# Long-run loads for x and w_out, weights of the first matmul read with a stride of four, and a reordered start

## The chip, the cores and the metric

The kernel runs on one core of a Trainium2 chip. The metric is the device time of one execution in microseconds, and the median of several executions is compared. A profile comes from one such execution.

The core has a matrix engine (TensorE, PE in the profile, with its weight loads apart as PEld), a vector engine (VectorE, DVE), a scalar engine (ScalarE, ACT), GpSimd (POOL) and a queue engine (SyncE, SP). SP and POOL issue DMAs here, and only those of POOL change the type on the way ("casting DMAs").

## The reference, cut to what matters

```python
# x: 8 x 4096 x 192, weight: 8 heads x 7 taps, w_in: 192 x 2048, w_out: 2048 x 192, all float32
w = softmax(weight)                               # over the 7 taps (with 1e-9 in the divisor)
conv[b, s, d] = sum_k w[head(d), k] * x_padded[b, s + k, d]     # 6 zero rows before each sequence
h = conv.reshape(32768, 192) @ w_in
out = maximum(0.01 * h, h) @ w_out                # 32768 x 192, float32
```

A short causal convolution with one set of taps for each of 8 heads is followed by a two-layer network with a leaky rectifier.

## The kernel before, in words

**Layout.** Two batch rows are worked on at once: they are r = 2p + e, with e = 0 on partitions 0 to 63 and e = 1 on 64 to 127. The 192 channels are three chunks of 64. So `xt` holds x with channels on partitions, three chunks and a halo of 16 columns, in bf16. A block is 512 positions of such a pair of rows, and there are 32 blocks (`NBLK`). The first five blocks are worked in two halves of 256 positions each (`HT`), the other 27 whole; `groups` is the list of these pieces. "Half 0" to "half 3" below are the first four groups; halves 0 and 1 are block 0, halves 2 and 3 are block 1.

**Getting x.** For most blocks, `load_x` brings x as bf16 into `x_bf` by six casting DMAs of POOL, one for each chunk and row, and `transpose_x` turns it by DMA transposes on SP into `xt`. The first four halves go another way, since the start cannot wait for that. `load_first` (L108) brings float32 rows by SP into `x_nat`, with one DMA for each of the two rows, 128 rows to a slab and one row of 768 bytes to a partition and slab. `cast_first` (L126) makes bf16 of it on DVE or ACT, `transpose_first` (L141) turns it on TensorE in twelve pieces into PSUM (`ptr`), and `evac_first` (L155) copies it to `xt`.

**The convolution.** `conv_jobs` makes the taps on DVE: for each chunk one multiply (L174) and six multiply-adds (L180), into `yt`. For half 0, chunks 0 and 1, and half 1, chunk 0, `pe_conv_jobs` does it on TensorE instead: 28 matmuls with diagonal weights (L199), two of them for each of 7 taps and two parts of the taps' precision. A scaling takes them out of PSUM, on ACT (`act_scale`, L328) for half 0 and on DVE (L205) for half 1.

**The two matmuls.** `mm1` makes one "unit" u: 12 matmuls of 256 columns (two feature groups of 128) in a half, or 6 of 512 in a whole block. Each pair runs on the two halves of the array's rows. ACT applies the rectifier and writes `g` (L372). The tile `ph` has two buffers, so TensorE can be two units ahead of ACT. `mm2_slot` makes two matmuls of the second product from `g` and `w_out` (L391); a fixed quota of slots follows each pair of units ("step" j), for groups that are already done. Outputs are taken from PSUM by `evac_o` (L438) and stored by SP. Two outputs are built together in two rounds with a change of array halves between them; the copy of the previous pair's second output stands as a seal between the rounds (`seal_round`). PSUM tiles for `ptr`, the convolution's `acc` and the outputs `po` share four buffers.

**Order.** The order of each engine's instructions is the order of the program text (`tc.manual_schedule()`). In half 0 (i = 0) there is no second product yet; there the taps of half 1 run, and the loads of halves 2 and 3 are let go behind the activations of units 0 and 6, by a dependence that is put in by hand. In half 1 (i = 1) half 3 is cast on ACT behind units 2 and 3 and turned after step 1. POOL's later loads wait behind a small copy (`pjunk`, L494) that reads the last `g` of half 0:

```python
if i == 1 and j == 1:
    nc.gpsimd.tensor_copy(out=pjunk, in_=g[0][0:1, NFC - 1, 1, HT - 1 : HT])
    load_x(2)
```

At the start SP issues the taps and the four loads of halves 0 and 1. POOL builds the selection matrix, then issues w_in in four casting DMAs (L236) and w_out in one (L241). TensorE is kept busy with matmuls of zeros (`warm`, L248) while it waits.

Of the kernel before, what the change touches and what calls it, by code (L numbers as in the profile page):

```python
# [9 lines left out]
FP32 = mybir.dt.float32  # L10
BF16 = mybir.dt.bfloat16
# [3 lines left out]
def kernel(  # L15
# [8 lines left out]
    nc = tc.nc  # L24

    B, S, D = x.shape
# [8 lines left out]
    CH = 64  # L35
    NCH = D // CH
    ST = 512
    SUB = ST // 128
    HT = ST // 2
    HS = SUB // 2  # L40
    NFC = F // 128
    NB = S // ST
    NBLK = (B // 2) * NB
    NHALF = 5
    NPEC = 2

# [15 lines left out]
    groups = [(b, h * HT, HT) for b in range(NHALF) for h in range(2)]  # L62
# [39 lines left out]

    def load_first(q, after=None):
        t = stage_pool.tile([128, 2, HS, D], FP32, name="x_nat")
        for e in range(2):
            ins = nc.sync.dma_start(  # L108
                out=t[:, e, :, :],
                in_=x[e, q * HT : (q + 1) * HT, :].rearrange("(c p) d -> p c d", p=128),  # L110
            )
            if after is not None and e == 0:
                tc.add_manual_dep(
                    ins.ins, after.ins.name,
                    mybir.DependencyInfo(
                        mybir.DependencyClass.Sync, mybir.DependencyReason.DATA
                    ),
                    reason="leave the DMA engines to the weights",
                )
        x_nat[q] = t  # L120

    def cast_first(q, e, copy):
        if q % 2 == 0 and e == 0:
            x_bf[q // 2] = xb_pool.tile([128, NCH, SUB, 2, CH], BF16, name="x_bf")
        h = q % 2
        copy(  # L126
            out=x_bf[q // 2][:, :, h * HS : (h + 1) * HS, e, :],
            in_=x_nat[q][:, e, :, :].rearrange("p s (c k) -> p c s k", c=NCH),
        )

# [2 lines left out]
    def transpose_first(q):  # L133
        ts = [
            psum_o.tile([128, HS, NCH, CH], BF16, name=f"ptr{i}", tag="po") for i in range(2)
        ]
        for s in range(HS):
            for c in range(NCH):
                for i in range(2):
                    ps = slice(i * CH, (i + 1) * CH)  # L140
                    nc.tensor.transpose(  # L141
                        out=ts[i][:, s, c, :],
                        in_=x_bf[q // 2][ps, c, (q % 2) * HS + s, :, :].rearrange(
                            "p e k -> p (e k)"
                        ),
                        identity=ident[ps, ps],
                    )
        ptr[q] = ts

    def evac_first(q, *copies):  # L150
        dst = xt[0][:, :, HALO + q * HT : HALO + (q + 1) * HT].rearrange(
            "p c (s i k) -> p i s c k", s=HS, i=2
        )
        for i, t in enumerate(ptr.pop(q)):
            copies[i](out=dst[:, i], in_=t)  # L155
# [78 lines left out]
    for fs in (slice(0, F // 2), slice(F // 2, F)):  # L234
        for e in range(2):
            nc.gpsimd.dma_start(  # L236
                out=w_in[e * CH : (e + 1) * CH, :, fs],
                in_=moe_w_in[:, fs].rearrange("(c p) f -> p c f", p=CH),
            )
    w_out = const_pool.tile([128, NFC, D], BF16)  # L240
    nc.gpsimd.dma_start(out=w_out, in_=moe_w_out.rearrange("(c p) d -> p c d", p=128))  # L241


    wa = psum_h.tile([128, 2, ST], FP32, name="warm", tag="ph")

    def warm(n):
        for _ in range(n):
            nc.tensor.matmul(  # L248
                out=wa[:, 0, 0:HT], lhsT=zero[:, 0:128], rhs=zero, start=True, stop=True
            )  # L250


# [102 lines left out]
    def mm1(grp, u):  # L355
        blk, t0, T = grp
        y = yt[blk]
        nf = ST // T
        ph = psum_h.tile([128, 2, ST], FP32, name="ph", tag="ph")
        for i in range(nf):  # L360
            f = nf * u + i
            for c in range(NCH):
                for e in range(2):
                    ps = slice(e * CH, (e + 1) * CH)
                    nc.tensor.matmul(  # L365
                        out=ph[:, e, i * T : (i + 1) * T],
                        lhsT=w_in[ps, c, f * 128 : (f + 1) * 128],
                        rhs=y[ps, c, t0 : t0 + T],
                        start=(c == 0),
                        stop=(c == NCH - 1),  # L370
                    )
        act = nc.scalar.activation(  # L372
            out=g[blk][:, nf * u : nf * (u + 1), :, t0 : t0 + T],
            in_=ph.rearrange("p e (i t) -> p i e t", i=nf),
            func=mybir.ActivationFunctionType.Prelu, alpha=0.01,
        )
        return act
# [66 lines left out]
            )  # L444
        return ins

    pjunk = const_pool.tile([1, 1], BF16)
    slot, avail = 0, 0
    for i, grp in enumerate(groups):
        blk, t0, T = grp  # L450
        steps = T // 64
        if t0 == 0:
            g[blk] = g_pool.tile([128, NFC, 2, ST], BF16, name="g", tag="g")
        quota = (avail - slot) // steps

        if i == 0:
            ahead = []
        else:
            ahead = conv_jobs(groups[i + 1]) if i + 1 < len(groups) else []
        per = -(-len(ahead) // steps)  # L460
        for j in range(steps):
            for u in range(2 * j, 2 * j + 2):
                act = mm1(grp, u)
                if i == 0 and u == 0:
                    pe_ahead, evac_y = pe_conv_jobs(groups[1], 0)
                    ahead = conv_jobs(groups[1], range(1, NCH))
                    per = len(ahead)
                if i == 0 and u == 3:
                    for job in pe_ahead:
                        job()  # L470
                if i == 0 and u in (0, 6):
# [24 lines left out]
            if i == 2 and j == 1:  # L496
                transpose_x(2)
            for job in jobs:
                job()
            if i == 1 and j == 1:  # L500
                transpose_first(3)
                evac_first(3, nc.vector.tensor_copy, nc.vector.tensor_copy)

            last_half = t0 + T == ST
            if j == steps // 4 and last_half:
                load_x(blk + 3)
            if j == steps // 2 and last_half and blk > 0:
                transpose_x(blk + 2)
        avail += 2 * T // 128 * NFC
# [36 lines left out]
```

## Time and profile before

| what | value |
|---|---|
| time, median of 3 runs | 695.6 us (695.6 to 696.04) |
| the profiled execution, time | 695.24 us |
| the profiled execution, span from first to last instruction | 693.5 us |
| granted TensorE clock | 1.000 |
| TensorE busy | 683.7 us, 99% of the span |
| VectorE, ScalarE, GpSimd busy | 543.9, 516.4, 139.7 us |
| DMA | 54.39 MB in 184015 packets |

The span is shorter than the execution's time by what lies before the first and after the last instruction. Busy shares are means over stages with different limits, so a stage must be read by itself: which wait ends last there. A row of a view names the line, the engine, the operation, the tiles written and read, and how often (x); in brackets stands how long the engine sat idle before it and what ended that. DMA-issuing instructions are not counted as busy.

### The profile page before, as it was taken

What the parts mean: (1) busy time and instruction counts of PE and PEld (TensorE: products, weight loads), DVE (VectorE), ACT (ScalarE), POOL (GpSimd) and SP (SyncE); (2) the same over time, 40 slices, a digit from 0 to 9 for tenths busy, and PEclk for the clock granted to TensorE, in tenths of its full rate; (3) what the DMA queues carried; (4) which work ended last, traced back from release to release, by engine and by line L of the source; (5) the groups of instructions that cost most, each with busy time, mean ns of one, the idle gap of its engine ahead of it and who ended that gap; (6) DMA issues with size and microseconds to landing.
All of it is one profiled execution on the core that took longest, in us unless ns stands there. A gap on an engine that the chain in (4) does not pass through costs nothing.

```text
span 693.5 us, 26049 instructions
## 1 busy us (share of the span) xinstructions
PE 683.7 (99%) x11778; PEld 539.4 (78%) x11778; DVE 543.9 (78%) x1005; ACT 516.4 (74%) x577; POOL 139.7 (20%) x195
## 2 busy tenths in 40 slices
PE   7999999999999999999999999999999999999997
PEld 5899998677777777777777777777777777777777
DVE  7899998977878787878787878877878878777812
ACT  6788888977777777777777777777777777777771
POOL 3632201502222202222112222102222022000000
PEclk9999999999999999999999999999999999999999
DMA  9995535935566345565355564545655365222112
GB/s 169 122 103 81 88 66 79 92 75 74 67 93 81 68 82 69 73 87 82 68 80 77 75 82 82 77 67 80 80 82 81 70 82 68 62 60 62 45 36 70
DMA packets 184015, 54.39 MB, mean 78 GB/s; under 512 B 148320, under 2 KB 183136, under 8 KB 183904
## 3 DMA queue, kind: packets, MB, share of 16 engines
q0 software_dynamic: 97936, 14.17, 30.3%
q1 hardware_dynamic: 85968, 38.56, 22.4%
q8 instruction: 92, 1.51, 1.0%
q14 instruction: 19, 0.16, 0.1%
HBM read 29.88 MB, written 25.17 MB: 79 GB/s over the span
## 4 chain that ended last, share of the span: by engine, by line
PE 93%; DMA 3%; DVE 2%; ACT 1%; POOL 0%; issue 0%; SPq 0%; POOLq 0%; DVEq 0%
PE po L391 48%; PE ph L365 45%; DVE yt L180 2%; DMA w_in<-in_moe_w_in_dram 1%; DMA x_nat<-in_x_dram 1%; DMA xt<-x_bf 1%; ACT g L372 0%; POOL sel L226 0%; DVE yt L174 0%; ACT x_bf L126 0%; POOL w_in L236 0%; PE ptr L141 0%; DVE x_bf L126 0%; SPq L441 0%; POOL sel L224 0%
## 5 line engine op out<-in xcount | busy, mean ns | idle before, releaser
L372 ACT ACTIVATE g<-ph 128x1024 bf16<-128x1024 f32 x512 | 496.2, 1021 | 156.2 <-PE ph L365 155.8
L180 DVE SCALAR_TENSOR_TENSOR yt<-xt,wk,yt 128x512 bf16<-128x512 bf16 (+1 forms) x648 | 442.3, 683 | 17.6
L391 PEld LDWEIGHTS <-g 64*128 64x128 bf16 (+1 forms) x8064 | 352.2, 94 | 45.3 <-issue 0.2
L391 PE MATMUL po<-w_out,g 64*128 64x192 bf16 (+1 forms) x8064 | 382.7, 243 | 0.0
L365 PE MATMUL ph<-yt,w_in 64*128 64x512 bf16 (+1 forms) x3552 | 379.3, 347 | 2.7 <-DMA w_in<-in_moe_w_in_dram 1.1
L365 PEld LDWEIGHTS <-w_in 64*128 64x128 bf16 x3552 | 186.5, 94 | 98.1 <-issue 4.6
L77 POOL DMA_DIRECT2D x_bf<-in_x_dram x180 | 133.7, 774 | 422.1 <-DMA xt<-x_bf 419.7
L438 DVE COPY o_sb<-po 128x192 f32<-128x192 f32 x216 | 77.1, 357 | 121.5 <-PE po L391 115.5
L174 DVE TENSOR_SCALAR yt<-xt,wk 128x512 bf16<-128x512 bf16 (+1 forms) x108 | 37.5, 347 | 2.0 <-DMA xt<-x_bf 1.9
L438 ACT COPY o_sb<-po 128x192 f32<-128x192 f32 x40 | 12.8, 320 | 1.9
L248 PE MATMUL warm<-zero 128*128 128x256 bf16 x24 | 4.8, 348 | 1.1 <-DVE junk L216 1.1
L199 PE MATMUL acc<-xt,diag 64*64 64x256 bf16 x84 | 5.2, 270 | 0.5 <-DVE xt L155 0.5
L199 PEld LDWEIGHTS <-diag 64*64 64x64 bf16 x84 | 4.3, 106 | 1.2 <-DVE xt L155 0.8
L303 ACT ACTIVATE diag<-ident,whm 128x64 bf16<-128x64 bf16 x14 | 3.5, 335 | 1.9 <-DVE whm L289 1.9
L248 PEld LDWEIGHTS <-zero 128*128 128x128 bf16 x24 | 2.4, 118 | 2.1 <-DVE junk L216 1.1
L494 POOL COPY pjunk<-g 1x1 bf16<-1x1 bf16 x1 | 0.2, 176 | 16.0 <-ACT g L372 16.0
L126 DVE CAST x_bf<-x_nat 128x384 bf16<-128x384 f32 x5 | 2.3, 454 | 1.4 <-DMA x_nat<-in_x_dram 1.4
L141 PE MATMUL ptr<-ident,x_bf 64*128 64x64 bf16 x48 | 1.4, 191 | 1.8 <-ACT x_bf L126 0.9
L141 PEld LDWEIGHTS <-x_bf 64*128 64x128 bf16 x48 | 1.0, 95 | 2.8 <-ACT x_bf L126 2.2
L236 POOL DMA_DIRECT2D w_in<-in_moe_w_in_dram x4 | 2.6, 660 | 0.0
L155 DVE COPY xt<-ptr 128x384 bf16<-128x384 bf16 x7 | 2.2, 351 | 0.5 <-PE ptr L141 0.4
L253 ACT ACT_TABLE_LOAD x1 | 1.3, 1283 | 0.8 <-PEq L530 0.8
(35 smaller groups left out, 12.9 us busy)
## 6 DMA issues: line engine op xcount, KB each, us to landing
out_dram<-o_sb SPq DMA_DIRECT2D x128, 192.0 KB, 2.1
x_bf<-in_x_dram POOLq DMA_DIRECT2D x180, 64.0 KB, 3.4
x_nat<-in_x_dram SPq DMA_DIRECT2D x8, 192.0 KB, 4.0
w_in<-in_moe_w_in_dram POOLq DMA_DIRECT2D x4, 384.0 KB, 9.7
xt<-x_bf SPq DMA_TRANSPOSE x90, 2.6
w_out<-in_moe_w_out_dram POOLq DMA_DIRECT2D x1, 768.0 KB, 16.3
w<-in_weight_dram SPq DMA_DIRECT2D x1, 0.2 KB
```

What stands on the lines that cost most here:

```text
L77: nc.gpsimd.dma_start(out=t[:, c, :, e, :], in_=src[2 * rp + e, :, :, c * CH : (c + 1) * CH],)
L141: nc.tensor.transpose(out=ts[i][:, s, c, :], in_=x_bf[q // 2][ps, c, (q % 2) * HS + s, :, :].rearrange("p e k -> p (e k)"), identity=ident ...
L174: lambda s=src, d=dst, c=c: nc.vector.tensor_scalar_mul(d, s, wk[:, c, 0:1])
L180: lambda s=src, d=dst, c=c, k=k: nc.vector.scalar_tensor_tensor(out=d, in0=s, scalar=wk[:, c, k : k + 1], in1=d, op0=mybir.AluOpType.mult, ...
L199: lambda k=k, p=p, a=a, e=e, ps=ps: nc.tensor.matmul(out=acc[ps, :T], lhsT=diag[c][ps, p, k, :], rhs=xt[0][ps, c, a : a + T], start=(k == ...
L236: nc.gpsimd.dma_start(out=w_in[e * CH : (e + 1) * CH, :, fs], in_=moe_w_in[:, fs].rearrange("(c p) f -> p c f", p=CH),)
L248: nc.tensor.matmul(out=wa[:, 0, 0:HT], lhsT=zero[:, 0:128], rhs=zero, start=True, stop=True)
L303: nc.scalar.activation(out=diag[c][:, 1, k, :], in_=ident2, func=mybir.ActivationFunctionType.Copy, scale=whm[:, c, 1, k : k + 1],)
L365: nc.tensor.matmul(out=ph[:, e, i * T : (i + 1) * T], lhsT=w_in[ps, c, f * 128 : (f + 1) * 128], rhs=y[ps, c, t0 : t0 + T], start=(c == 0) ...
L372: act = nc.scalar.activation(out=g[blk][:, nf * u : nf * (u + 1), :, t0 : t0 + T], in_=ph.rearrange("p e (i t) -> p i e t", i=nf), func=my ...
L391: return nc.tensor.matmul(out=po[m], lhsT=g[b][ps, fc, e, s * 128 : (s + 1) * 128], rhs=w_out[ps, fc, :], start=start, stop=stop,)
L438: ins = copy(out=o_sb[:, n % 2, :], in_=po.pop(n))
```

## The change

The rows of x for halves 0 to 3 are dealt to partitions two at a time: partition p takes positions 2p and 2p + 1, which lie side by side in memory (1536 bytes), and one DMA brings both batch rows. Evacuation to `xt` then writes every second column. Halves 0 and 1 still come by SP as float32 and are cast. Half 2 comes by one casting DMA of POOL into `x_rows` and is turned in 24 smaller pieces. Half 3 comes by six casting DMAs into `x_half3` in the layout that the transposes read. POOL's queue now holds, in order, w_in, half 2, w_out, half 3 and block 2, with no wait between them.

w_out is dealt four rows at a time (`RUN = 4`): partition p takes the features 512 c + 4 p + i, which lie side by side in memory (3072 bytes). To match, `mm1` picks the columns of w_in with a stride of four.

Half 1's casts move from DVE to ACT, behind the two scalings of half 0. Its transposes move from before the first unit to behind it, its 28 taps on TensorE are spread over units 2 to 5, and its scaling moves to ACT. Half 2 is turned behind unit 6. Half 3 is turned after step 2 of half 1, not after step 1. A few warm matmuls are added. The helper's argument `after`, the copy to `pjunk` and the casts of halves 2 and 3 go.

```diff
+    RUN = 4
...
-    def load_first(q, after=None):
-        t = stage_pool.tile([128, 2, HS, D], FP32, name="x_nat")
-        for e in range(2):
-            ins = nc.sync.dma_start(
-                out=t[:, e, :, :],
-                in_=x[e, q * HT : (q + 1) * HT, :].rearrange("(c p) d -> p c d", p=128),
-            )
-            if after is not None and e == 0:
-                tc.add_manual_dep(
...
-        x_nat[q] = t
+    x_half = {
+        q: const_pool.tile([128, NCH, HS, 2, CH], BF16, name=f"x_half{q}") for q in (0, 1, 3)
+    }
+    x_rows = const_pool.tile([128, 2, HS, D], BF16, name="x_rows")
+
+    def load_first(q):
+
+        rows = x[0:2, q * HT : (q + 1) * HT, :].rearrange("e (p s) d -> p e (s d)", s=HS)
+        if q < 2:
+            x_nat[q] = stage_pool.tile([128, 2, HS, D], FP32, name="x_nat")
+            nc.sync.dma_start(out=x_nat[q].rearrange("p e s d -> p e (s d)"), in_=rows)
+        elif q == 2:
+            nc.gpsimd.dma_start(out=x_rows.rearrange("p e s d -> p e (s d)"), in_=rows)
+        else:
+            for c in range(NCH):
+                for e in range(2):
+                    nc.gpsimd.dma_start(
+                        out=x_half[q][:, c, :, e, :],
+                        in_=rows[:, e].rearrange("p (s d) -> p s d", s=HS)[
+                            :, :, c * CH : (c + 1) * CH
+                        ],
+                    )
...
-                    nc.tensor.transpose(
-                        out=ts[i][:, s, c, :],
-                        in_=x_bf[q // 2][ps, c, (q % 2) * HS + s, :, :].rearrange(
-                            "p e k -> p (e k)"
-                        ),
-                        identity=ident[ps, ps],
-                    )
+                    if q != 2:
+                        nc.tensor.transpose(
+                            out=ts[i][:, s, c, :],
+                            in_=x_half[q][ps, c, s, :, :].rearrange("p e k -> p (e k)"),
+                            identity=ident[ps, ps],
+                        )
+                        continue
+                    for e in range(2):
+                        nc.tensor.transpose(
+                            out=ts[i][e * CH : (e + 1) * CH, s, c, :],
+                            in_=x_rows[ps, e, s, c * CH : (c + 1) * CH],
+                            identity=ident[ps, ps],
+                        )
...
-            "p c (s i k) -> p i s c k", s=HS, i=2
+            "p c (i k s) -> p i s c k", s=HS, i=2
...
+    load_first(2)
+
+
     w_out = const_pool.tile([128, NFC, D], BF16)
-    nc.gpsimd.dma_start(out=w_out, in_=moe_w_out.rearrange("(c p) d -> p c d", p=128))
+    nc.gpsimd.dma_start(
+        out=w_out.rearrange("p (c i) d -> p c i d", i=RUN),
+        in_=moe_w_out.rearrange("(c p i) d -> p c i d", p=128, i=RUN),
+    )
+    load_first(3)
+    load_x(2)
...
-    warm(5)
+    warm(7)
+    warm(1, 128)
...
-    for n, job in enumerate(conv_jobs(groups[0], range(NPEC, NCH))):
-        if n in (4, 5):
-            cast_first(1, n - 4, nc.vector.tensor_copy)
+    for job in conv_jobs(groups[0], range(NPEC, NCH)):
         job()
     for c in range(NPEC):
         pe_jobs, evac_y = pe_conv_jobs(groups[0], c)
         for job in pe_jobs:
             job()
         evac_y(act_scale)
+        cast_first(1, c, nc.scalar.copy)
         if c == 0:
             warm(2)
-    transpose_first(1)
-    evac_first(1, nc.vector.tensor_copy, nc.vector.tensor_copy)
...
-                        lhsT=w_in[ps, c, f * 128 : (f + 1) * 128],
+                        lhsT=w_in[
+                            ps, c, bass.DynSlice(f // RUN * RUN * 128 + f % RUN, 128, RUN)
+                        ],
...
-                act = mm1(grp, u)
+                mm1(grp, u)
                 if i == 0 and u == 0:
+                    transpose_first(1)
+                    evac_first(1, nc.vector.tensor_copy, nc.vector.tensor_copy)
                     pe_ahead, evac_y = pe_conv_jobs(groups[1], 0)
                     ahead = conv_jobs(groups[1], range(1, NCH))
                     per = len(ahead)
-                if i == 0 and u == 3:
-                    for job in pe_ahead:
+                if i == 0 and 2 <= u <= 5:
+
+                    n = len(pe_ahead) // 4
+                    for job in pe_ahead[(u - 2) * n : (u - 1) * n]:
                         job()
-                if i == 0 and u in (0, 6):
-                    load_first(2 + u // 6, act)
-                if i == 1 and u in (2, 3):
-                    cast_first(3, u - 2, nc.scalar.copy)
+                if i == 0 and u == 5:
+                    evac_y(act_scale)
+                if i == 0 and u == 6:
+                    transpose_first(2)
...
             if i == 0 and j == 3:
-                evac_y(nc.vector.tensor_scalar_mul)
-                for e in range(2):
-                    cast_first(2, e, nc.vector.tensor_copy)
-                transpose_first(2)
                 evac_first(2, nc.vector.tensor_copy, nc.vector.tensor_copy)
-            if i == 1 and j == 1:
-
-                nc.gpsimd.tensor_copy(out=pjunk, in_=g[0][0:1, NFC - 1, 1, HT - 1 : HT])
-                load_x(2)
...
-            if i == 1 and j == 1:
+            if i == 1 and j == 2:
                 transpose_first(3)
                 evac_first(3, nc.vector.tensor_copy, nc.vector.tensor_copy)
```

More of the change, by code (lines that the diff above doesn't have):

```diff
@@ L101, in new_xt @@
         nc.vector.memset(xt[rp][:, :, 0:HALO], 0.0)
-    def load_first(q, after=None):
-        t = stage_pool.tile([128, 2, HS, D], FP32, name="x_nat")
-        for e in range(2):
-            ins = nc.sync.dma_start(
-                out=t[:, e, :, :],
-                in_=x[e, q * HT : (q + 1) * HT, :].rearrange("(c p) d -> p c d", p=128),
-            )
-            if after is not None and e == 0:
-                tc.add_manual_dep(
-                    ins.ins, after.ins.name,
-                    mybir.DependencyInfo(
-                        mybir.DependencyClass.Sync, mybir.DependencyReason.DATA
-                    ),
-                    reason="leave the DMA engines to the weights",
-                )
-        x_nat[q] = t
+    x_half = {
[18 more added lines that the diff above has]
+                    )
     def cast_first(q, e, copy):
-        if q % 2 == 0 and e == 0:
-            x_bf[q // 2] = xb_pool.tile([128, NCH, SUB, 2, CH], BF16, name="x_bf")
-        h = q % 2
         copy(
-            out=x_bf[q // 2][:, :, h * HS : (h + 1) * HS, e, :],
+            out=x_half[q][:, :, :, e, :],
             in_=x_nat[q][:, e, :, :].rearrange("p s (c k) -> p c s k", c=NCH),
@@ L140, in transpose_first @@
                     ps = slice(i * CH, (i + 1) * CH)
-                    nc.tensor.transpose(
-                        out=ts[i][:, s, c, :],
-                        in_=x_bf[q // 2][ps, c, (q % 2) * HS + s, :, :].rearrange(
-                            "p e k -> p (e k)"
-                        ),
-                        identity=ident[ps, ps],
-                    )
+                    if q != 2:
[11 more added lines that the diff above has]
+                        )
         ptr[q] = ts
@@ L239, with warm @@
             )
+    load_first(2)
     w_out = const_pool.tile([128, NFC, D], BF16)
-    nc.gpsimd.dma_start(out=w_out, in_=moe_w_out.rearrange("(c p) d -> p c d", p=128))
+    nc.gpsimd.dma_start(
[4 more added lines that the diff above has]
+    load_x(2)
     wa = psum_h.tile([128, 2, ST], FP32, name="warm", tag="ph")
-    def warm(n):
+    def warm(n, cols=HT):
         for _ in range(n):
             nc.tensor.matmul(
-                out=wa[:, 0, 0:HT], lhsT=zero[:, 0:128], rhs=zero, start=True, stop=True
+                out=wa[:, 0, 0:cols], lhsT=zero[:, 0:128], rhs=zero[:, 0:cols],
+                start=True, stop=True,
             )
@@ L285 @@
     select(wps_l, 2)
-    warm(5)
+    warm(7)
+    warm(1, 128)
     new_xt(0)
@@ L445, in evac_o @@
         return ins
-    pjunk = const_pool.tile([1, 1], BF16)
     slot, avail = 0, 0
```

## The prediction

> **What bounds the kernel now.** I read the page's first part, then busy time by stretch, then the chain that ended last and the timeline of the first 35 us, which give the place and size of every wait.
>
> ```profile
> PE 683.7 (99%) x11778; PEld 539.4 (78%) x11778; DVE 543.9 (78%) x1005; ACT 516.4 (74%) x577; POOL 139.7 (20%) x195
> ```
> ```profile
> 33.80:118.00 84.20, 84.20 (x1800) 79.66 (x1796) 79.06 (x168) 72.23 (x97) 20.20 (x28) 1.00 0.61 84
> 136.00:677.00 541.00, 541.00 (x9108) 413.97 (x9106) 418.76 (x733) 401.48 (x415) 95.59 (x129) 1.00 0.49 73
> ```
> In the stretches the columns are length, then busy us of PE, PEld, DVE, ACT, POOL, clock and DMA. TensorE has no hole at all from 33.8 to 118 and from 136 to 677; between them it lacks 0.5 us (17.51 of 18), and the tail after 677 is the last output. So the time moves in two ways only: the dense stream starts earlier or later, or its own pace changes.
>
> ```profile
> 3.65 8.95 DMA w_in<-in_moe_w_in_dram
> 12.64 0.84 PE ph L365 x11
> 13.51 1.03 ACT g L372
> 14.97 6.26 DMA x_nat<-in_x_dram
> 21.25 0.44 DVE x_bf L126
> 26.58 0.40 ACT x_bf L126
> 27.91 0.41 ACT x_bf L126
> 28.36 0.35 PE ptr L141 x12
> ```
> This is the chain (start, length, what). The first matmul waits until w_in lands at 12.6; half 2's x is let go only behind the first g (13.5) and lands at 21.2; half 3's cast stands in ACT's line between two g's.
>
> ```profile
> 14.58 1.75 PE L365 MATMUL ph<-yt,w_in 64*128 64x256 bf16 x24 [0.46 <-ACT g L372]
> 16.26 1.72 PE L199 MATMUL acc<-xt,diag 64*64 64x256 bf16 x28
> 19.86 1.75 PE L365 MATMUL ph<-yt,w_in 64*128 64x256 bf16 x24 [0.46 <-ACT g L372]
> 21.91 1.63 PE L365 MATMUL ph<-yt,w_in 64*128 64x256 bf16 x24
> 28.36 0.35 PE L141 MATMUL ptr<-ident,x_bf 64*128 64x64 bf16 x12 [0.86 <-ACT x_bf L126]
> 33.81 0.93 PE L365 MATMUL ph<-yt,w_in 64*128 64x256 bf16 x14
> 6.09 0.60 DVE L318 TENSOR_SCALAR rsum<-wraw 128x3 f32<-128x3 f32 x1
> 33.52 0.49 DVE L174 TENSOR_SCALAR yt<-xt,wk 128x256 bf16<-128x256 bf16 x1
> ```
> Half 1's matmuls start at 21.91, half 2's at 33.81. DVE finishes half 2's y at 33.52, so there DVE is only 0.3 us ahead. That moment, 33.81, is my yardstick: everything after it is dense and follows it one for one.
>
> [...] No strided weight is in the trace before; it shows 94 ns per load, and that loads keep up with the second matmul's pace of 1.32 us for 16 pairs, 82 ns. [...] the 128x3 multiply at 6.09 took 0.60 us and ended as POOL's w_out issue did (5.51 + 1.20), while the two-input taps took the same 3.09 us for six with POOL issuing and without. [...] from 5 to 6 us x's packets take 38.0% of the engines and w_in's 59.5%.
>
> **The change, part by part.**
> *Loads of halves 0, 1* (SP): four issues become two, runs 768 to 1536 bytes. x still occupied 0.38 us of all engines after 5.0 us, when w_in's packets begin. I expect x to be through by then: w_in lands 0.45 earlier, 12.15 (bounds 0 and 0.9: nothing, or all of x's remaining share plus fewer stragglers). POOL issues w_in as before.
> *Casts of half 1* leave DVE (0.42 + 0.43, so chunk 2 of y is ready at 10.9, not 11.72) for ACT (2 x 0.5, one after each scaling). ACT's last scaling ends at 11.18 + 0.47 = 11.65, its second cast at 12.17. All are before 12.15 or level with it: hidden by w_in's landing. Three more warm matmuls and two small ones are covered by waits (TensorE idles from 5.1 to 5.9); the small one ahead of the first selection may cost 0.05.
> *Half 1's transposes* move behind the first unit of matmuls. Before, DVE could begin half 1's taps at 12.29. Now: 12.15 + 12 matmuls at 54.5 ns (24 took 1.31) = 12.80, transposes 0.35 = 13.15, two evacuations 0.62 = 13.80. Behind DVE's wait stand half 1's taps, half 2's evacuation and half 2's taps.
> *Half 1's taps on TensorE*: one block of 28 (1.72 us) held ACT from 17.39 to 18.78. Four parts of 0.43 alternate with units of 0.65. Two units ahead of ACT is the limit (two ph buffers), so ACT runs nearly through: 12.85 + 8 x 0.97 + 0.45 for the scaling it takes from DVE = 21.1, perhaps 21.2 with half 2's 24 transposes (12 cost 0.35; I take 0.5, bounds 0.3 and 1.2).
> *Half 1's matmuls*: y's chunk 2 comes from DVE at 13.80 + 6.72 (12.29 to 19.01) = 20.55; the second unit needs ACT's last g at 21.2. First mm2 at 21.85 against 23.37.
> *Halves 2, 3*: three DVE casts or scalings (0.48 + 0.42 + 0.43) and two ACT casts (0.50 each) go, and both waits on x (0.61, 0.80). The 0.86 wait ahead of half 3's transposes goes; but moved to the end of step 2 they take PSUM that output 1 leaves, and that copy is sealed behind the round's last mm2: 0.55 by the row of such a copy (31.39 + 0.32 against mm2's end near 31.18).
> *POOL's queue*: w_out's issue (1.20 us) should shrink with its runs (2048 to 512); it is moved behind one load (about 0.7), then follow 6 + 6 loads at 0.77, to about 17. Landing: w_out took 16.3 us from 5.51, to 21.8. At 16 us 505 of its packets moved in 1 us, so 2048 take 4.1; that is 388 GB/s read, and I don't expect longer runs to beat it (bounds: 3 and 4.1). Half 2's 384 KB ahead of it add 1.0, the old loads of half 2 on SP beside it (0.7, in proportion to their 2 x 192 KB) are gone, w_in is 0.45 earlier: 21.8 + 1.0 - 0.7 - 0.45 = 21.65, wanted at 21.85. That is close; half 3's 1536 short packets at 700 per us (4203 in 6 us from 25) add 2.2: 23.9, needed at 28.4. Block 2's x follows, needed near 37. Removing the gate on POOL (0.18 copy) costs nothing.
> *Stride of four*: 3552 weight loads. [...] bounds 0 and the second rival's. A gain is excluded, for the loads already hide under matmuls.
>
> **Sum.** DVE path: 20.55, half 2's evacuation 0.67, half 2's taps with half 3's evacuation as before (22.77 to 33.50, 10.75) = 31.97; two or three multiplies slowed by POOL (0.28 to 0.50) = 32.15. Four matmuls can precede chunk 2 (0.22): dense from 31.93. TensorE path: 21.85 + 1.31 + 2 x 2.63 = 28.42, PSUM wait 0.55, transposes 0.25, last step 2.63 = 31.85. They meet within 0.1, so I take 32.0: 33.81 - 32.0 = **1.8 us earlier**. The profiled run took 695.24 (span 693.5 and 1.74 around it), so 693.4 by it; the median is 695.6, 0.36 above, and on it the forecast is **693.8**. A measurement here tells 0.2%, 1.4 us, from no change.
>
> **Rivals.**
> *Given back, same.* w_in is held by its slowest engine, not by x, and lands at 12.6; POOL's steady issuing delays more DVE work; the 24 transposes cost 1.2. Each takes 0.2 to 0.7 of the 1.8: gain 0.3 to 1.3, 694.3 to 695.3. For it: w_in lands at 12.6 though x is nearly done by 6. Against: both x waits and one 0.86 wait vanish whatever w_in does.
> *Stride costs, slower.* If a strided load needs more than 82 ns, the first load after each mm2 run is late; there are 36 such in the half blocks and 8 x 27 in the full ones, 252. At 108 ns: 252 x 0.026 = 6.6 us, net 700. At 164 ns also the half blocks' 480 pairs, paced at 109 ns, slip by 55: 21 + 26 = 47 us, 741. It decides from 89 ns on (1.8 us). For it: no such row before[...].
> *Transfers late, slower.* w_out or half 3 comes late on a lagging engine (the engines' share falls to 0.53 from 19 us on, yet w_out lands at 21.8). From w_out at 23.7 the gain is gone; at 26 it is 2 us slower, 698. Against: fewer packets in all, no SP loads beside them, and a forecast landing 0.2 ahead of need.
>
> **How the numbers follow.** Forecast 0.60 (gain 1.0 to 2.7, 692.9 to 694.6; 0.50 of it beyond 0.2%); given back 0.16 (0.02 faster, 0.13 same, 0.01 slower); late transfers 0.10 (0.03 same, 0.07 slower); stride 0.14, slower. Faster 0.52, same 0.26, slower 0.22. The range leaves out the stride and a few of the others: 692.6 to 696.8.
>
> **What would show it.** Right: first mm1 unit complete near 12.8; no ACT wait inside half 0; first mm2 near 21.9; dense TensorE from about 32, with DVE ending half 2's y beside it; weight loads of w_in still under an unchanged 1.31 us per 24 matmuls. Wrong: that 1.31 grows, mm2 waits on w_out, or TensorE waits on a ptr after 29.

## The result, and the profile after

The changed kernel is slower by 0.6%. Its median is 700.24 us (699.61 to 701.01, 6 runs), beside 695.82 us for the kernel before in the same comparison (6 runs). The ratio is 1.0062, with a 95% interval of [1.0049, 1.0075]. The profiled execution took 701.01 us, span 699.3 us, which is 5.8 us more than the span before.

The page's first part and the busy time by stretch, read as before:

```profile
PE 688.2 (98%) x11794; PEld 587.4 (84%) x11794; DVE 544.8 (78%) x1000; ACT 517.4 (74%) x578; POOL 144.3 (21%) x201
```
```profile
12.00:16.00 4.00, 0.52 (x5) 0.28 (x7) 0.00 (x0) 0.00 (x0) 1.22 (x2) 0.86 1.17 207
16.00:20.00 4.00, 4.00 (x47) 2.74 (x45) 2.51 (x6) 2.10 (x3) 1.47 (x2) 0.50 1.50 188
...
142.00:683.00 541.00, 541.00 (x9109) 453.21 (x9107) 418.55 (x732) 401.41 (x415) 95.74 (x129) 1.00 0.48 73
```

The last row is the one to look at first. In 541 us of whole blocks TensorE does 9109 matmuls. Before, it did 9108 in the same length, although weight loading (the second busy figure) rose from 414 to 453 us. The long steady part has not changed its pace. What has changed is ahead of 40 us: from 12 to 16 us TensorE does 5 matmuls and VectorE and ScalarE do nothing, and then the granted clock (third figure from the right) falls to 0.50.

The chain of work that ended last shows what the start hangs on:

```profile
4.88 10.85 DMA w_in<-in_moe_w_in_dram
15.73 0.05 issue
15.78 1.09 PE ph L385 x7
...
35.74 0.33 ACT o_sb L460
36.07 0.04 issue
36.11 0.52 PE ptr L148 x11
```

It is the w_in transfer issued at 4.88, which lands at 15.73; in the kernel before, the chain ran through one issued at 3.65. The timeline of TensorE and VectorE gives each wait in brackets:

```profile
10.92 0.30 PE L385 MATMUL ph<-yt,w_in 64*128 64x256 bf16 x1
11.55 0.30 PE L385 MATMUL ph<-yt,w_in 64*128 64x256 bf16 x1 [0.33 <-DMA w_in<-in_moe_w_in_dram]
13.79 0.30 PE L385 MATMUL ph<-yt,w_in 64*128 64x256 bf16 x1 [1.95 <-DMA w_in<-in_moe_w_in_dram]
15.78 1.25 PE L385 MATMUL ph<-yt,w_in 64*128 64x256 bf16 x9 [1.69 <-DMA w_in<-in_moe_w_in_dram]
17.34 1.07 DVE L167 COPY xt<-ptr 128x384 bf16<-128x384 bf16 x2 [6.28 <-PE ptr L148]
36.11 0.52 PE L148 MATMUL ptr<-ident,x_half 64*128 64x64 bf16 x11 [0.41 <-ACT o_sb L460]
39.08 1.64 PE L385 MATMUL ph<-yt,w_in 64*128 64x256 bf16 x24
```

The first four matmuls of the first unit start one by one at 10.92, 11.55, 13.79 and 15.78, three of them after a wait for w_in. The kernel issues w_in in four transfers: two for columns 0 to 1023 and two for 1024 to 2047. The first unit multiplies by columns 0 to 511 only, so it needs the first two. It had both by 11.55, earlier than I forecast, and then waited 3.6 us more. Half 1's transposes are queued behind this unit, so VectorE stood idle for 6.28 us. Half 2's matmuls start at 39.08 instead of 33.81, 5.3 us late.

### The profile page after: what moved, and what is told of

It is laid out like the page before. It is cut to its first block, busy times and chain, and to the rows that moved or that the text cites. A ratio compares the mean times of both kernels' runs of the same rounds, so it can differ in the third digit from the quotient of the medians.

```text
span 699.3 us, 26075 instructions
## 1 busy us (share of the span) xinstructions
PE 688.2 (98%) x11794; PEld 587.4 (84%) x11794; DVE 544.8 (78%) x1000; ACT 517.4 (74%) x578; POOL 144.3 (21%) x201
## 4 chain that ended last, share of the span: by engine, by line
PE 91%; DVE 5%; DMA 2%; ACT 1%; POOL 1%; issue 0%; POOLq 0%
PE po L413 46%; PE ph L385 45%; DVE yt L192 4%; DMA w_in<-in_moe_w_in_dram 2%; ACT g L394 1%; PE acc L211 0%; DVE yt L186 0%; POOL w_in L248 0%; POOL sel L238 0%; PE ptr L148 0%; POOL sel L236 0%; DVE o_sb L460 0%; ACT o_sb L460 0%; PE ptr L155 0%; POOL ident masks.py:199 0%
## 5 line engine op out<-in xcount | busy, mean ns | idle before, releaser
L385 PE MATMUL ph<-yt,w_in 64*128 64x512 bf16 (+1 forms) x3552 | 387.6, 349 | 5.3 <-DMA w_in<-in_moe_w_in_dram 4.0
L413 PEld LDWEIGHTS <-g 64*128 64x128 bf16 (+1 forms) x8064 | 361.6, 94 | 33.3 <-issue 0.2
L413 PE MATMUL po<-w_out,g 64*128 64x192 bf16 (+1 forms) x8064 | 387.7, 243 | 0.0
L385 PEld LDWEIGHTS <-w_in 64*128 64x128 bf16 x3552 | 230.3, 110 | 68.6 <-DMA w_in<-in_moe_w_in_dram 4.5
L167 DVE COPY xt<-ptr 128x384 bf16<-128x384 bf16 x7 | 3.8, 583 | 7.5 <-PE ptr L148 6.3
L268 PE MATMUL warm<-zero 128*128 128x256 bf16 (+1 forms) x28 | 5.2, 340 | 1.1 <-DVE junk L228 1.1
L124 POOL DMA_DIRECT2D x_half<-in_x_dram x6 | 4.3, 711 | 5.5 <-DMA w_in<-in_moe_w_in_dram 5.5
L148 PE MATMUL ptr<-ident,x_half 64*128 64x64 bf16 x36 | 1.8, 207 | 0.9 <-DVE wraw L338 0.5
L148 PEld LDWEIGHTS <-x_half 64*128 64x128 bf16 x36 | 1.4, 105 | 1.4 <-ACT x_half L132 0.7
L351 ACT ACTIVATE yt<-acc,rsum 128x256 bf16<-128x256 f32 x3 | 1.4, 465 | 0.5 <-PE acc L211 0.5
## 6 DMA issues: line engine op xcount, KB each, us to landing
w_out<-in_moe_w_out_dram POOLq DMA_DIRECT2D x1, 768.0 KB, 14.1
```

What stands on the lines that cost most here:

```text
L124: nc.gpsimd.dma_start(out=x_half[q][:, c, :, e, :], in_=rows[:, e].rearrange("p (s d) -> p s d", s=HS)[:, :, c * CH : (c + 1) * CH],)
L268: nc.tensor.matmul(out=wa[:, 0, 0:cols], lhsT=zero[:, 0:128], rhs=zero[:, 0:cols], start=True, stop=True,)
L385: nc.tensor.matmul(out=ph[:, e, i * T : (i + 1) * T], lhsT=w_in[ps, c, bass.DynSlice(f // RUN * RUN * 128 + f % RUN, 128, RUN)], rhs=y[ps, ...
L413: return nc.tensor.matmul(out=po[m], lhsT=g[b][ps, fc, e, s * 128 : (s + 1) * 128], rhs=w_out[ps, fc, :], start=start, stop=stop,)
```

## The experiments

The theory was: the stride makes the program wait in the first unit for parts of w_in that it doesn't read, and everything else is small. The rivals: the transfers are late because of the new order; the clock's fall is the loss; the strided copies to `xt` are; the strided weight read is.

**1. w_in as two tiles, the stride kept.** The two halves of the columns are stored in tiles of their own, so that a wait for one need not take in the other. Same elements, same transfers.

```diff
-    w_in = const_pool.tile([128, NCH, F], BF16)
+    w_in = [const_pool.tile([128, NCH, F // 2], BF16, name=f"w_in{n}") for n in range(2)]
...
-                        lhsT=w_in[
-                            ps, c, bass.DynSlice(f // RUN * RUN * 128 + f % RUN, 128, RUN)
+                        lhsT=w_in[f // 8][
+                            ps, c, bass.DynSlice(f % 8 // RUN * RUN * 128 + f % RUN, 128, RUN)
```

> Theory (false wait): with the stride, the third and fourth weight loads of the first unit are made to wait for the two w_in transfers of the upper 1024 features, which they do not read. Here w_in is two tiles, so they cannot. Expected: first unit complete near 12.3 us and not 17; TensorE clock 1.0 throughout; half 2's matmuls start near 32.9 (12.3, transposes 0.3, two strided evacuations 1.07, half 1's taps 6.75, again 1.1, half 2's taps with half 3's evacuation 11.5), against 33.8 before and 39.1 in the changed kernel: about 694.8 us. Rival (the stride itself: loads of 110 ns, not 94): the dense stream is slower per matmul, and the time stays near 700.

Measured: 694.91 us, ratio to the kernel before 0.9989 [0.9982, 0.9995]. In its timeline:

```profile
11.42 0.87 PE L385 MATMUL ph<-yt,w_in 64*128 64x256 bf16 x11 [0.21 <-DMA w_in<-in_moe_w_in_dram]
22.43 1.51 PE L413 MATMUL po<-w_out,g 64*128 64x192 bf16 x32
33.52 1.28 PE L385 MATMUL ph<-yt,w_in 64*128 64x256 bf16 x20 [0.53 <-DVE yt L192]
```

The first unit runs through at 11.42 after a wait of 0.21 us. It reads the same columns with the same stride, so the two later waits of the changed kernel were for data that it doesn't use. This one edit gives back 5.3 us of medians and turns a loss into a gain of 0.1%.

**2. No stride, the rest of the change kept.** Contiguous columns of w_in, and w_out in its old short runs.

```diff
...
-                        lhsT=w_in[
-                            ps, c, bass.DynSlice(f // RUN * RUN * 128 + f % RUN, 128, RUN)
-                        ],
+                        lhsT=w_in[ps, c, f * 128 : (f + 1) * 128],
```

> The changed kernel with w_in read without a stride and w_out loaded in 768-byte runs as before; all else of the change stays. False wait: the same recovery as with two tiles, about 694.8 us, or up to 1 us more if w_out in short runs lands after 22 and holds the first mm2. Stride itself: also recovers, so this run alone does not tell the two apart, together with two tiles it does. Rival (the start's new order is to blame, not the stride): stays near 700.

Measured: 694.56 us, 0.9985 [0.9979, 0.9992]; first unit from 11.43, half 2's matmuls at 32.47 with no wait. Without the stride the loss is gone as well, with the new order and the strided copies to `xt` still there.

**3. The stride alone, in the kernel before.** The kernel before with strided columns of w_in and w_out in long runs.

```diff
...
-                        lhsT=w_in[ps, c, f * 128 : (f + 1) * 128],
+                        lhsT=w_in[
+                            ps, c, bass.DynSlice(f // RUN * RUN * 128 + f % RUN, 128, RUN)
+                        ],
```

> The kernel before with only the stride and w_out's long runs. False wait: the first unit waits for the fourth w_in transfer, 16.4 us where it waited to 12.6; half 0 starts 3.7 later, TensorE idles over 4 us and its clock drops; half 1's taps are not behind it here. Expected 3 to 5 us slower than before, 699 to 701. Stride itself: slower by the pace of all 3552 loads, with the first unit at 12.6. Rival (new order to blame): as before, 695.7.

Measured: 700.29 us, 1.0067 [1.0055, 1.0079]. The same two waits stand in its timeline, in the old order of work:

```profile
14.11 0.30 PE L369 MATMUL ph<-yt,w_in 64*128 64x256 bf16 x1 [1.27 <-DMA w_in<-in_moe_w_in_dram]
16.14 4.46 PE L369 MATMUL ph<-yt,w_in 64*128 64x256 bf16 x45 [1.74 <-DMA w_in<-in_moe_w_in_dram]
```

So the loss comes with the stride and needs nothing of the new order. The rival of late transfers falls. (w_out's long runs are part of this edit too; experiment 4 keeps them and loses nothing.)

**4. The stride in the kernel before, with two tiles.** Experiment 3 with the tiles of experiment 1: is there a cost of the strided read itself?

```diff
...
-                        lhsT=w_in[ps, c, f * 128 : (f + 1) * 128],
+                        lhsT=w_in[f // 8][
+                            ps, c, bass.DynSlice(f % 8 // RUN * RUN * 128 + f % RUN, 128, RUN)
+                        ],
```

> The kernel before with the stride and w_out's long runs, and w_in in two tiles. False wait: first unit at 12.6 as before, clock 1.0, 695.6 within 0.5; the loads' 110 ns stay hidden under 1.31 us per 24 matmuls. Stride itself: some us slower than before.

Measured: 695.68 us, 1.0000 [0.9991, 1.0008]. The group of weight loads, and in the timeline the starts of half 1's last step and of half 2's first:

```profile
L369 PEld LDWEIGHTS <-w_in 64*128 64x128 bf16 x3552 | 229.5, 110 | 63.7 <-issue 5.0
```
```profile
31.50 1.47 PE L369 MATMUL ph<-yt,w_in 64*128 64x256 bf16 x24
34.13 1.47 PE L369 MATMUL ph<-yt,w_in 64*128 64x256 bf16 x24
```

A strided load is recorded with 110 ns, a contiguous one with 94. The next step of 24 and 32 matmuls still starts 2.63 us later, as before (31.18 and 33.81). The read itself costs nothing that the measurement can tell; the wait is all of it.

**5. Forty warm matmuls ahead of the first unit.** They keep TensorE busy while it waits, for about as long as the wait.

```diff
+    warm(40)
     g, po, osb, seal = {}, {}, {}, None
```

> The changed kernel with 40 more matmuls of zeros (107 ns each, 4.3 us) ahead of the first unit, so that TensorE is not idle while it waits for w_in. If the clock drop (0.5 from 16 to 21 us) is a cost of its own, the clock stays 1.0, units of half 0 take 0.65 and not 1.2, and the time falls by 1 to 2.5 us to 698 to 699; the wait to 15.8 stays. If the clock drop is hidden behind ACT's pace, no change.

Measured: 698.59 us, 1.0044 [1.0032, 1.0056]. All five runs lie below all six of the changed kernel. By stretch, and the first unit in the timeline:

```profile
12.00:16.00 4.00, 4.00 (x44) 3.47 (x44) 0.00 (x0) 0.00 (x0) 0.98 (x2) 1.00 1.18 208
16.00:20.00 4.00, 3.72 (x68) 2.77 (x62) 3.34 (x8) 3.39 (x4) 1.21 (x2) 1.00 1.53 185
```
```profile
10.92 4.54 PE L268 MATMUL warm<-zero 128*128 128x256 bf16 x40
15.39 0.84 PE L386 MATMUL ph<-yt,w_in 64*128 64x256 bf16 x12
```

The granted clock stays at 1.00, and from 16 to 20 us TensorE does 68 matmuls, not 47. VectorE and ScalarE still idle from 12 to 16 (0.00). The matmuls of zeros hold the first unit until 15.39, about when w_in's last transfer lands in this run (4.88 + 10.6), so the wait keeps its length within some 0.4 us. So of the 5.3 us between the changed kernel and experiment 1, about 1.65 (700.24 - 698.59) are the clock, by this estimate. The other 3.7 are the wait itself, which the timelines of those two give as 3.97 - 0.21 = 3.76.

**6. What the strided copies to `xt` cost.** With w_in in two tiles, each copy writes whole runs. This leaves out that the two positions of a pair are put side by side.

```diff
-            "p c (i k s) -> p i s c k", s=HS, i=2
+            "p c (s i k) -> p i s c k", s=HS, i=2
...
```

> The two-tile kernel with the evacuations writing whole runs, as before the change; it leaves out that the positions of a pair of rows are put side by side. Theory: 0.35 us per evacuation, DVE 1.4 us earlier, 693.5 us. Rival (evacuations are off the path): 694.9.

Measured: 693.65 us, 0.9970 [0.9958, 0.9981], 1.26 us less than experiment 1. The group of these copies on the page after, and then on that of this run:

```profile
L167 DVE COPY xt<-ptr 128x384 bf16<-128x384 bf16 x7 | 3.8, 583 | 7.5 <-PE ptr L148 6.3
```
```profile
L167 DVE COPY xt<-ptr 128x384 bf16<-128x384 bf16 x7 | 2.2, 351 | 2.4 <-PE ptr L148 2.4
```

A copy with every second column written takes 583 ns, a plain one 351, the figure of the kernel before too. Three pairs stand on VectorE's path to half 2's y: 6 x 0.23 = 1.4 us. The profiled execution took 694.65 us, longer than five of the other six runs, and shows less of the gain: its first unit waited for ScalarE's y until 11.86, and half 2's matmuls start at 32.91, 0.6 us before those of experiment 1.

**7. The same copies with the loops turned**, so that the write is in runs and the read of PSUM is strided.

```diff
-            copies[i](out=dst[:, i], in_=t)
+            copies[i](
+                out=dst[:, i].rearrange("p s c k -> p c k s"),
+                in_=t.rearrange("p s c k -> p c k s"),
+            )
...
```

> The two-tile kernel with the evacuation's loops in another order: each pair of neighbouring columns of xt is written one after the other, and PSUM is read at the stride instead. Theory: the evacuations of the changed kernel take 0.58 us and not 0.35 because xt is written every second column; read at a stride they fall back to about 0.35, DVE is 3 x 0.46 = 1.4 us earlier at the end of half 2's y and at the seam to the whole blocks near 118 us, where TensorE waits for DVE: 693.5 us. Rival: the stride costs the same on the PSUM side: 0.58, 694.9.

Measured: 694.77 us, 0.9985 [0.9978, 0.9992], with copies of 553 ns on VectorE, a pair in 1.02 us where experiment 1 takes 1.06 and experiment 6 0.62. There the cost moves from the written side to the read side and hardly shrinks. The one copy of this kind on ScalarE does get its old price back: 478 ns in the kernel before, 587 with every second column written, 478 here.

**8. Long runs of x alone, in the kernel before.** Halves 0 to 3 come in one SP transfer each of 1536-byte runs, with the strided copies that this needs.

```diff
-        for e in range(2):
-            ins = nc.sync.dma_start(
-                out=t[:, e, :, :],
-                in_=x[e, q * HT : (q + 1) * HT, :].rearrange("(c p) d -> p c d", p=128),
-            )
...
+        ins = nc.sync.dma_start(
+            out=x_nat[q].rearrange("p e s d -> p e (s d)"),
+            in_=x[0:2, q * HT : (q + 1) * HT, :].rearrange("e (p s) d -> p e (s d)", s=HS),
+        )
...
```

> The kernel before with the four loads of halves 0 to 3 by one DMA each in runs of 1536 bytes, still by SP and still cast, with the strided evacuation that this needs. Theory: long runs of x are why w_in's second transfer landed at 11.5 and not 12.6; it lands near 11.6 here, half 0 starts 1.0 earlier, two evacuations ahead of half 2's y cost 0.46 each: 695.0 to 695.7. Rival: w_in lands at 12.6 as before (what helped it in the changed kernel was another thing), and the evacuations make it 1 us slower, 696.6.

Measured: 696.28 us, 1.0008 [1.0000, 1.0017]. On w_in's landing it is inconclusive: in the profiled execution the 28 matmuls of the first convolution took 2.61 us, not 1.72, so the first unit could start only at 12.35 and then waited for ACT's y; w_in had landed by then, and when is not seen. On the copies it is clear: VectorE is behind, and half 2's matmuls wait 0.78 us for it at 35.03.

**9. The new order alone.** Experiment 2 with x in the old short runs and plain copies, so that neither stride is left.

```diff
-        rows = x[0:2, q * HT : (q + 1) * HT, :].rearrange("e (p s) d -> p e (s d)", s=HS)
+        rows = x[0:2, q * HT : (q + 1) * HT, :].rearrange("e (s p) d -> p e s d", s=HS)
...
-            "p c (i k s) -> p i s c k", s=HS, i=2
+            "p c (s i k) -> p i s c k", s=HS, i=2
...
```

> The changed kernel without stride and without long runs: x of halves 0 to 2 and w_out in runs of 768 bytes, each row's load by itself, whole-run evacuations; the new order of the start, the casting loads in line and the taps in parts stay. Theory: the order is the gain, the long runs of x cost 3 x 0.46 on DVE and bring at most 0.5 to 1 through an earlier w_in. Evacuations 0.35, w_in complete between 11.6 and 12.6: 693.2 to 694.0, that is 0.6 to 1.4 better than without stride but with long runs (694.56). Rival: the earlier w_in is worth as much as the evacuations cost: 694.6.

Measured: 694.95 us, 0.9987 [0.9979, 0.9995]. I had expected 693.2 to 694.0. The timeline says where part of that went:

```profile
12.29 0.83 PE L382 MATMUL ph<-yt,w_in 64*128 64x256 bf16 x11 [1.31 <-DMA w_in<-in_moe_w_in_dram]
33.29 1.49 PE L382 MATMUL ph<-yt,w_in 64*128 64x256 bf16 x24
```

With short runs of x, the first unit gets w_in at 12.29 and not at 11.43 (experiment 2). One execution of each says little, for the landing varies. But over all traces here in which a matmul waited for these transfers, it came at 11.84 to 13.17 with short runs of x (five traces) and at 11.42 to 11.55 with long ones (three). So the long runs gain something at the start, 0.3 to 1.8 us by these figures, and lose about 1.3 in the copies (experiment 6). The two medians, 694.95 and 694.56, can't be told apart.

**10. Long runs of w_out on top**, with the stride and two tiles.

```diff
...
+        out=w_out.rearrange("p (c i) d -> p c i d", i=RUN),
+        in_=moe_w_out.rearrange("(c p i) d -> p c i d", p=128, i=RUN),
...
```

> The order-alone kernel with the stride, w_out in runs of 3072 bytes and w_in in two tiles. If w_out's long runs are worth anything, mm2 starts earlier or the time falls by over 0.4 against order alone; theory: w_out lands some 1 us earlier but nobody waits for it, same time within 0.4.

Measured: 695.19 us, 0.9993 [0.9986, 0.9999], level with experiment 9. w_out takes 13.6 us from issue to landing instead of 14.7, and no matmul waits for it in either; a later load of POOL does, for 2.9 us in experiment 9 and 2.4 here.

**11. Half 3 turned earlier, on experiment 9.** Behind step 1, with its second copy by ACT.

```diff
-            if i == 1 and j == 2:
+            if i == 1 and j == 1:
                 transpose_first(3)
-                evac_first(3, nc.vector.tensor_copy, nc.vector.tensor_copy)
+                evac_first(3, nc.vector.tensor_copy, nc.scalar.copy)
```

> The order-alone kernel with half 3 turned after step 1 again and one of its two evacuations on ACT. The wait of half 3's transposes for the output copy (0.41 us beside 0.19 of their own) goes, and DVE has 0.31 less: if DVE sets the seam near 118 us, 0.3 better than order alone; if TensorE does, 0.5 better; if half 3's x lands after 26 us, a new wait there, and no gain.

Measured: 694.35 us (693.13 to 696.51), 0.9978 [0.9969, 0.9987]. The wait for PSUM ahead of half 3's transposes is gone. This is the lowest median of the whole computation here, but its interval overlaps those of experiments 2 and 9, so it can't be called faster than they are. In its profiled execution w_in came at 13.17, with the same loads as experiment 9 and 0.88 us later.

**12. The same edit on experiment 2**, where x comes early.

> The changed kernel with contiguous weights of w_in and w_out in short runs (as in the run without the stride, 694.56), and half 3 turned behind step 1 of half 1, its second evacuation by ACT. Theory (the false wait is gone, what is left is DVE's work up to half 2's y and up to the seam near 118 us): the 0.40 us wait for PSUM before half 3's transposes goes and one strided evacuation of 0.53 us leaves DVE; half 2's matmuls start near 32.0, and the seam wait of 0.57 falls below 0.3: 694.0, 693.8 to 694.3. Rival (the strided copy on ACT stands between two g's and stops TensorE, or the seam takes what was gained): 694.4 to 694.8.

Measured: 694.80 us, 0.9986 [0.9979, 0.9993], no better than experiment 2. The wait for PSUM went, and half 2's matmuls start at 31.95 instead of 32.47. Then, at the first whole block, in this run and (second fence) in experiment 2:

```profile
118.48 1.04 PE L382 MATMUL ph<-yt,w_in 64*128 64x512 bf16 x8 [1.39 <-DVE yt L192]
```
```profile
117.91 1.04 PE L382 MATMUL ph<-yt,w_in 64*128 64x512 bf16 x8 [0.57 <-DVE yt L192]
```

TensorE waits there for VectorE's y, and being further ahead it waits longer. The rival was right about the time: nothing is left of the gain at the seam. Why VectorE itself comes 0.57 us later there, with one copy less to do, was not tested. Its 26 multiplies of 128x256 between 13 and 118 us took 8.3 us in this run and 7.6 in experiment 2, which is as much as that copy was worth.

## Why the prediction was wrong, point by point

**The first unit: the step that failed.** I wrote that the first unit is complete at "12.15 + 12 matmuls at 54.5 ns (24 took 1.31) = 12.80". The transfers that it needs landed at 11.55, better than the 12.15. But the unit waited for all four transfers and ended near 17.0. The stride was bounded as a rate only, with "bounds 0 and the second rival's" for the 3552 weight loads. The sum takes the 0, which was my estimate, since no strided weight stands in the trace before, and the wait was put at nothing without a reason. The prediction looks for added waits where the change moves lines, not where it changes an operand's shape. Experiments 1 to 4 show that the wait comes from the stride on one tile and goes with two tiles.

Why the program waits is read, not measured. The two false waits stand at the third and fourth matmul (13.79 and 15.78 us), the first that read chunk 1 of the channels; the first two, on chunk 0, wait for no transfer that they do not read. In a partition's row of w_in, chunk 1's columns 0 to 511 lie between the pieces that an upper transfer fills in chunks 0 and 1; chunk 0's lie ahead of them all. My estimate, from these places alone, is a dependence test that, for a strided slice, compares whole stretches from first to last element. No run here singles it out.

**The clock.** No step priced a TensorE idle for 4 us. In the changed kernel TensorE was busy for 0.52 of the 4 us from 12 to 16 (5 matmuls), and the granted clock was 0.50 from 16 to 20, 0.57 from 20 to 22 and 1.00 from 22 on. In experiment 3, behind waits of 1.27 and 1.74 us, it was 0.73 from 16 to 18, 0.50 from 18 to 20 and 0.92 from 20 to 22. In experiment 1, with a wait of 0.21 us, and in experiment 5, with matmuls in the wait, it stayed at 1.00. By experiment 5 this made the wait about 1.65 us dearer.

**The taps in parts.** The prediction alternates parts of 0.43 us with units of 0.65, so that ScalarE sets the pace. Experiment 1 shows:

```profile
14.18 0.62 PE L211 MATMUL acc<-xt,diag 64*64 64x256 bf16 x7
14.73 0.85 PE L385 MATMUL ph<-yt,w_in 64*128 64x256 bf16 x12
15.51 0.62 PE L211 MATMUL acc<-xt,diag 64*64 64x256 bf16 x7
```

A part takes 0.55 us to the next start and a unit 0.78, 1.33 together and not 1.08. So TensorE sets the pace here, and ScalarE waits 0.31 us three times. The first mm2 started at 22.43, not 21.85, although the first unit was complete 0.5 us earlier than forecast.

**The copies.** I took "two evacuations 0.62", from the row of the kernel before, though the change writes every second column. They measured 1.07. The forecast without the false wait can be checked against experiment 1: VectorE's end of half 2's y was forecast at 32.15. The first copies start at 12.48 instead of 13.15 (-0.67), three pairs of copies cost 3 x 0.45 more (+1.35), and the two multiplies that met POOL's issuing took 0.61 and 0.66, not 0.28, where I had allowed 0.2 in all (+0.5). That makes 33.33; y was used at 33.52. With the prediction's own 0.22 for the four matmuls that can precede it, TensorE would be dense from 33.11, and the gain 0.7 rather than 1.8 even with the wait removed. Experiment 1's median is 0.7 below that of the kernel before. The slowed multiplies are what the rival "given back" named, "POOL's steady issuing delays more DVE work". (The operation at 6.09 that the prediction calls a multiply is an addition, L318; that it ended with POOL's issue is read rightly.)

**"Everything after it is dense and follows it one for one."** This failed as well. Until the first whole block TensorE can run ahead of VectorE only so far. The table sets half 2's start beside the start of the fifth matmul of the first whole block, and the span. In the kernel before and in experiment 9 the twelve matmuls of that unit run through without a wait, and a third of their time (1.53 and 1.56 us to the next group) is added to their start:

```profile
117.97 1.71 PE L365 MATMUL ph<-yt,w_in 64*128 64x512 bf16 x12
```
```profile
117.45 1.74 PE L382 MATMUL ph<-yt,w_in 64*128 64x512 bf16 x12
```

| kernel | half 2 starts | fifth matmul of the whole block | wait there | span less that | span less half 2's start |
|---|---|---|---|---|---|
| before | 33.81 | 118.5 | 0 | 575.0 | 659.7 |
| after | 39.08 | 124.76 | 0.75 | 574.5 | 660.2 |
| experiment 1 | 32.59, then 33.52 | 119.02 | 0.94 | 574.6 | 661.0 |
| experiment 2 | 32.47 | 117.91 | 0.57 | 574.5 | 659.9 |
| experiment 6 | 32.91 | 118.36 | 0.68 | 574.5 | 660.0 |
| experiment 9 | 33.29 | 118.0 | 0 | 574.6 | 659.3 |
| experiment 12 | 31.95, then 32.54 | 118.48 | 1.39 | 574.4 | 661.0 |

The last column but one stays within 0.6 us, the last varies by 1.7: what the span follows is the seam near 118 us, not half 2's start. Experiment 9 starts half 2 0.8 us later than experiment 2 and ends only 0.2 later; experiment 12 starts it 0.5 earlier and ends 0.5 later. Where a wait stands in the table, the seam is set by VectorE's work between the two. In the prediction's own row VectorE was busy 79.06 of 84.20 us there, and I read TensorE's missing holes as VectorE having room.

**What was right.** The wait on a `ptr` for PSUM was forecast at 0.55 and came at 0.41 us, with the copy `o_sb` that I named. The 24 transposes took 0.38 (forecast 0.5). w_out landed at about 20.3 (its issue at 6.24, and 14.1 to landing) and no matmul waited for it; forecast 21.65. The pace of 1.31 us per 24 matmuls held, as forecast, under loads of 110 ns instead of 94, which show that a strided load is not quite free. In the prediction's list of what would show it wrong, only "TensorE waits on a ptr after 29" came true, and that one was foreseen; the event that decided was not on the list.

The rival "stride costs" named the right edit and even the right size, 700, by a mechanism that the runs rule out, so that its hit on the size is luck: experiment 4 has the same strided loads and loses nothing.

## What to carry to other kernels

When an operand's slice changes its shape, ask what it now waits for as well as how fast it is read: a strided slice of a tile filled by several transfers can wait for all of them (3.97 us here), and two tiles kept the waits apart (0.21 us in experiment 1). Price a copy by its new access pattern, not by the row of the old one (583 ns here, not 351). When one engine starts earlier, follow the second busiest to the next place where the first needs it; the gain counts there (in experiment 12 a start 0.5 us earlier met a wait of 1.39 us near 118 us, where experiment 2 has 0.57).

## What the runs showed of the hardware that was not expected

- A 128x384 bf16 copy from PSUM to SBUF took 0.35 us in runs, 0.58 with every second element written, and 0.55 with the stride on the read side, on VectorE (351, 583 and 553 ns; pairs took 0.62, 1.06 and 1.02 us in experiments 6, 1 and 7). On ScalarE the three took 478, 587 and 478 ns, one copy each.
- A weight load of 64x128 bf16 with a stride of four shows 110 ns against 94, and 3552 of them cost no time that could be told (experiment 4, ratio 1.0000 [0.9991, 1.0008]).
- A VectorE multiply of 128x256 bf16 took longer at times while POOL issued loads. Of the 27 in the kernel before, the 19 with no such issue beside them took 0.28 to 0.29 us and the other 8 took 0.28 to 0.52; in the changed kernel these were 19 at 0.28 to 0.29 and 8 at 0.28 to 0.66. Which multiplies are met differs between runs. In experiment 2 the multiplies at 24.82 and 28.14 took 0.28 and 0.32 us, in experiment 1 the ones at 24.87 and 28.51 took 0.61 and 0.66. That alone is 0.67 us.
- POOL's later loads waited for older ones to land, though the kernel's text has no such wait (and "The change" says that there is none):

```profile
POOL x_half L124 <- DMA w_in<-in_moe_w_in_dram: 5.5, 4, 1.5
POOL x_bf L78 <- DMA w_out<-in_moe_w_out_dram: 3.0, 1, 3.0
```

Of the waits by engine in the changed kernel, half 3's loads stood 5.5 us behind w_in (four times, 1.5 at most), and block 2's 3.0 behind w_out. The first wait is that of POOL's ninth load for its first, w_in's, and w_out's is that of the fourteenth for the sixth: both stand behind the load eight places ahead. Whether the built program or the chip makes it wait, the profile doesn't say. Nothing on the path needed these loads sooner.
